# A block-sparse attention and gated feed-forward kernel: more buffers in eight tile groups, and a new order of all its instructions

## The chip, the cores and the metric

The kernel runs on one core of one Trainium2 chip. The metric is the device time of one execution in microseconds (us), as the median of several runs.

## The reference

The inputs are `q`, `k` and `v` of shape (4, 8, 768, 64), a table of sampled blocks, and the weights of a feed-forward layer. In short:

```python
scores = q @ k.T / 8                       # 4 batches, 8 heads, 768 x 768
mask   = near | first or last block row/column | 3 sampled blocks of 32 per block row
attn   = softmax(where(mask, scores, -1e9)) @ v
x      = heads side by side                # (4, 768, 512)
h      = relu(x @ w_in)                    # (4, 768, 1024)
gate   = sigmoid(conv3(h, conv_w))         # along the tokens, each feature by itself
out    = (h * gate) @ w_out                # (4, 768, 512)
```

## The kernel before

The batches are cut into halves of 384 query tokens, the last half again into 256 and 128, so that there are nine segments. The attention of a segment is cut into units of eight 128 x 128 score blocks; there are 144 units in all, numbered in the order of their exponentials. Two heads (a head pair) share a slot of tiles; there are 16 head pairs.

For each head pair, POOL's DMA queue loads keys and queries (`nat`, and `nq` for the second half of the queries of the first five pairs) and values (`vn`), with a cast to bf16. The first five pairs are transposed by TensorE into PSUM (`k_tr`, `q_tr`) and copied out by DVE or ACT; the later pairs are transposed by DMAs that SP issues (`xb`, into `stg`, L583) and copied by DVE (`stg_cp`). Both end in the tiles `e` and `o`, which also hold 24 rows that make the mask a part of the score matmul. The mask rows of slots 1 and 2 are copied by DVE, those of slots 3 and 4 by DMAs on SP (L359).

For each unit, PE makes the scores in two halves (`s`, L744, into one of two PSUM tiles `st`), ACT takes the exponential (`exp`, L755, into one of the `pt` tiles), and PE multiplies with V and a column of ones (`av`, L777). At the end of a head pair in a segment, DVE takes the reciprocal of the sums (`rcp`, L694) and normalises (`norm`, L696) into `xtok`; SP's DMA transposes that into `xT` (`x_xb`, L705), or PE does for a few (L715). When the four pairs of a segment are there, PE runs the first linear layer (`f1`, L893), ACT or DVE the relu (L913, L915), DVE the convolution (`mul`, `add`, L947, L957), ACT the tanh that stands for the sigmoid (L996), DVE the gate (`g1`, `g2`, L999, L1004), PE the second linear layer (`f2`, L823; L808 for the last 128 tokens), ACT or DVE the eviction (`ev`, L326 or L328, into `o2s`), and SP or ACT the store (L831, L817). One late segment's convolution runs on PE (L968), with diagonal matrices that DVE makes (`diag`, L388).

Nothing is scheduled when the program is built. All operations are collected in a graph, and a string `ORDER` is then replayed: two characters name an operation, one more its engine where there is a choice (P, A, V, G, S), and one more each buffer it takes. Each engine executes its own operations in the order of that string, and waits for operands and for the buffer's last reader.

```python
            o = ops[64 * CODE.index(line[x]) + CODE.index(line[x + 1])]
            ...
            if len(engines) > 1:
                e = ENGINES[line[x]]
            ...
            for b in o.allocs:
                b.index = CODE.index(line[x])
```

Loads on POOL are held back by small copies (`pace`): some read the loaded tile of three loads earlier (L658), the later ones an exponential (L415), so that a load is issued no earlier than that has happened. This rule is part of the graph, whatever the order.

The buffer counts stand in one line, from which the tiles are made:

```python
    NSLOT, NSTG, NNAT, NVN, NPT, NXK, NXT, NHE, NCV, NGT, NOS = 5, 2, 4, 3, 6, 3, 3, 2, 4, 2, 4
```

`NXK` counts two groups of tiles, `xtok` and `rcp`.

Of the kernel before, what the change touches and what calls it, by code (L numbers as in the profile page):

```python
# [25 lines left out]
1n15N05u5y5O5z05G0P470Q48241490R4a1A04b0S4c2604d274e0T4f2c24g1O14h2e14i2f4j2k04k2m34P05a4l2n4m5K35S15H5L5T5P4
5A25B5C1oV5U55/05M605Q6105R6415V5W656906a5X05Y25V41pV5Z05+V6616e16216fhr1ho06b26g36j0hp636khs0k0DhqV0htVhM06l4
6r1676s6t5hx0hyhzA6w06xhu1hv1B06y0hOhNhPhwVhQhU1hVhWhX6B16C686c6d6hhD16G0hE6H1CA1DA6D1hFAhA06i6m6n06O1hB1W16u
6P6v6z6I2hCAhRhY1XV46o1i021YV6pi16Q36T0hG06A6U6E6V4hH6F6Y16ZhJ16J6+56KhK710726R16S6WhZhLAhIA730i3hSi26L0i4hT0
i57611P1im06X6/1RV1QV777e01Z1707f747817j17k756M2806q1296Ni831+V1/Viah+2dV0h/i9ig17g27l37o07p797a07h7i7t17u7q4  # L30
i6ibi77b2ic7v5ih7B07C7D0id7m7n7r7s7G17w7x7Hin2lV12aV0io7L07M2g12h7I17N2ii7c7d7y12bV7z7E17Q17R7F7J7K7V07Wieifip
7O7S37A7X42s12u2v24n0IiqV0811827P7T7U860878358807Y7Z0ij8b18civ0iw8g08h7+02iV12jV2tV2ixV7/ikA1is1itiuViQ08d12o0
2p8i28o18p8q3iB08t0848uiC858v48y18z898a8e8f8D08E8j8kiy1iz8A58F12x2w2C2002F802iAAiRiSiTiDViU2qV2iV2rV8l2iY1iE0
8r18s8I18w8JiF8K0iGA8x8Q02118B8R8C8V18W8GiH0iI8H8S28X3iZi+22V8miW23Vi/8+08/904iXj0iJVj18LiK1iL931948M0iMVj42j5
8N1j7j28O8T9b08U8Y9ciN0iO8Z91iPVj39559g19h9d19i0jC19l09m9n3929697980jc3j6jdj8jfjejg999q19r9s59e19f9j9k9v09wjq0
9x19D19E9o9pjr9t9u9I0jD9y9J9z0j99F0jh9N19G9O9HjajbjijEjs9K59P02G02D22EV3jj2I2H2Q2N2R12O02y12z2J08n2K8P9a9S09T
jFjt9U2juA20L2LV39A2jGV32PV49B2MV2AV40K2BV9+19L9M9/a30a49QjI1jJa04jL0a819RjM9Va9a53jKA1jNA2/3032T2S2Yaa032ad0
aejU19Wa119X19YjX0k40jVai1a2jYaf1jWAk6jZVa6a7ajk11aq0abark2jO0acak2jPas5k5kk1k7kmjQAav1awaA0agahalaBjR0jSam0
ax4aC3k8k3Vklknan0j+1j/k0VkoaF1atjTAk9kc2aokdks3kfkakektkgkukb1aGaN0jk0auayaOaH0jlazaS1aTaP1kpaU5jw1jmaX0aYir
jHjv2U09C0il331aZ4khjxaDaEjnjoA0aIaJb01b1b23jyjzb50aQ1aRb6aVaWkA0jAA3b70kqaK22V2WV0kvkikwkjaLkxbd1a+bekG1a/b3  # L40
b4kBbi0bjkHb8b902Z131373820Map9Z34aMbf2bn1bo2XVkykrkCkzkD2+V0bk139V135V1bp536Vba0bb3a3b23f3c3d3ebs0kIbtkJkKV2
bA1kEA1kP0bBkQkM1kNkRVkOVl80l9lalblcbu4bC3bF0bGbgbhblbK1bLbmkS0bqbH0bM2bP0brbQkTbR1bU1kV1kWbVc00bvbwbD1bEc1ld
kUVkXVbx1lg2lhlelibyk/0bIbJbNbW5c23c51c6c70bOl0ca0cbbSbTbXbY0cf1cgkY1kZcc2ch5ljl1Vlklfk+VbZ2lllo13p3m3n03q03u
3r3g0bc1jp3hkFb+b/bzc3l20c4cn0cocp4l51l3l6cs1ctcx0l4Al7Acyc8c9lK0cdcecicjcu1cz3lplqlr3v1lw3lmlxlnlslylzcC1cD
cE0ltck0lAlucllvlE1cq1cH0lFcIcP1crcvcwcAcQcBcFlLcGcJ5cU0cKcL0cVlGlMlBcR4cW13s3E3t3B3F13J3G3H3C13I3Q3R2cmcScZ1
c+3iV2lClDlHlNd20d3cTc/2cXda1db3oV2lIV0cM2lOV1d43dc0m31cYd0m00d1m1m4cN3jVm2V0m5Adf0dgdk1dlm60m7dh5mo0mpm8Vdm4
mf1mgd5d6dp0dqdu1mc0mddr1meAmhAdd1jB3w3klP3K0cO23L3T3U33Y3V3W3Xdvdw2434403ldedC0dDml0mmm91mamnAdE3mr3xV4d71mq
3yVmsmE2dH1didImi0mjmFmGmbVmw1mxdJ0mkVmtd8djdM0dndodNlQ1dR1dSdslRdO5lSdtdxdZ0d+lTdT4mM3mHmz3DV3dz0mumydAmImv0
mAlUV3mNmOd/1e21e3dy0dFdGdKe70e42dLlW0lXdPdQe8ec1dUdVedmJmBe93lYlZe01m+1e1ee0mCdW2mDmPl+A1eh0eiej5e5e6m/eamU0
mVebep1eqeu0evmKmQdXmLmR3MV3mSmTn0mWn13Z1kL3+d93SV445V03/V0mXefegekdBlVdYl/3AlJer4ew1n2A2em13NVen40VmYA3ez1eA  # L50
eE0nd1eFeB2neeG3na0nbnfVncVnA0nBnCnDnE3PmZ3O3z41eo042eM1eNeO0el0n41eR0eSeT5n5n70n8eW1eseteXe/0exeyf0eCeDn6An9A
ns1eY4ng1nhf41eHeIf5nj0f11nFntnuniVeJ0nveKf62fc0nkfdfe3nwnlVnxnGnI2np1nqnJnrVnKnynLeP1fh1eQfinm0eUeVfm0eZfnnn
e+f2f3f7fj0fo5noAnznMnQ3nSnRnHf92nTfafr1f80fffsfgfkflfpfz0fAft4fB1nNnY1fE1fFo20fqfufvfJ0fKfG2fw1nUnOfL3nVfxnP
nZo3fR1fC1fDfHfSfIfMfW0fXfNn+o4fT0fY5eLfbfyf/1fU0g0nWg14nXo5o6V10Hg70g8n/fVfZgc1gdo0A0ok0olo7n3o1g91ge2fO0omV1
on1ooopVoI1oKgh0gioq0gp1gj3oJoLfPot1orosAgqouovAoQ0oRoToSgu0gvgr0oC0f+g2oF1oGoHAoDoEAgw5g3g42oUp42g5ga1gbgz1gA
oz1oAgfgggkglow0oxoBAgB4p5gm1oMgs0gnoyAoY3gtgxgyfQ1g6gogCgI0gJgDoNgN1gK1gOoe1ofogp6gE0gFoZo+gL1gG0gMgV0gP2gHV
o/oVp0oOoWohgQgWp7oP1gS2oiA3gR0po0ppgX3pqApA1gTp8h11h2pu1gYgZpvpx0pyh60h30pwApr1pspzAp1pBpCoXpQ0p2p3g+0pDg/ptA
p9papRpEpbpI3pJpLo80o9h7gU2h0hf1oaobhgh41h5h85ocA1pi1pjpkhh4plh9ha0hihjpc0pmA2pFhb1hchd1heAhk2pKhlpdpehm1pfpM
pNpgA0pGhnVqg1qhqiAqp0qqpHpY2pSpOpTqrAqj1qkqs1qtqm0qnqlAqu1qoAqx0qypPqz3pZp/pUpVp+qvq0phpnodojq1qa1qC1q40qDqH0
qIqwpWpXqJ1qE0q2qAqBq3qM0qbqcq5qFq6q7qdqeA0q8A2qfq9qKqGqLqNqOqPqQA1qRAqS1qTqUqVqWV3qXSqY0qZq+q/r0Ar1A  # L60
"""


# [49 lines left out]
def kernel(  # L113
# [210 lines left out]
    def dcopy(e, dst, src):  # L324
        if e == "ACT":
            nc.scalar.copy(out=dst, in_=src)  # L326
        else:
            nc.vector.tensor_copy(out=dst, in_=src)  # L328
# [732 lines left out]
```

## Time and profile before

| | |
|---|---|
| runs | 210.04, 211.36, 209.91 us; median 210.04 |
| profiled execution | span 207.2 us from the first to the last instruction |
| granted TensorE clock | 1.000 |
| PE, DVE, ACT, POOL busy | 95%, 88%, 91%, 29% of the span |
| DMA moved | 26.26 MB, mean 127 GB/s |

The time of a run is counted around the span; the profiled execution's own time is known only as its span. PE is TensorE's matmuls, PEld its weight loads, DVE the vector engine, ACT the scalar engine, POOL GpSimd, and SP the engine that only issues DMAs. A name like `st<-o,e` is the tile that is written and those that are read. L744 is line 744 of the kernel. "SPq" is SP's sequencer, issuing. In brackets stands how long an engine was idle before an instruction, and what ended that.

### The profile page before, as it was taken

The numbers are of one execution on the slowest core, as the hardware profiler recorded it, in microseconds if no ns is written. First come the engines' busy times: TensorE is split into PE (matmuls) and PEld (weight loads), VectorE is DVE, ScalarE is ACT, GpSimd is POOL, SyncE is SP. The second block draws the span as 40 slices with busy tenths as digits, with TensorE's granted clock in tenths as the row PEclk, the third lists the DMA queues.
The fourth block names the chain that finished last, engine by engine and source line by source line (L and its number), as shares of the span: only waits on it lengthen the run. The fifth ranks groups of instructions, "written<-read, shape, count | busy, mean of one in ns | idle before, by whom it ended". The sixth has DMA issues, their size and how long they took to land.

```text
span 207.2 us, 6783 instructions
## 1 busy us (share of the span) xinstructions
PE 196.7 (95%) x2667; PEld 153.7 (74%) x2687; DVE 181.5 (88%) x571; ACT 189.4 (91%) x248; POOL 60.7 (29%) x113
## 2 busy tenths in 40 slices
PE   7799979989999999999999999999999999999993
PEld 7689858867878877777688767777688877795752
DVE  6877759999699998999999998999799959999950
ACT  6899969999999999999999998999899999998841
POOL 8844355446326124500605292700000000000000
PEclk9999999999999999999999999999999999999999
DMA  6999999999998699993597689992511032100415
GB/s 149 170 207 200 173 169 126 141 135 157 158 151 134 98 138 194 181 190 58 77 167 133 88 103 218 170 213 73 175 43 22 19 121 66 29 11 6 156 50 202
DMA packets 54903, 26.26 MB, mean 127 GB/s; under 512 B 40864, under 2 KB 51832, under 8 KB 54872
## 3 DMA queue, kind: packets, MB, share of 16 engines
q0 software_dynamic: 19984, 11.24, 43.5%
q1 hardware_dynamic: 34312, 13.90, 33.8%
q10 hardware_dynamic: 576, 0.69, 1.0%
q8 instruction: 21, 0.34, 0.7%
q14 instruction: 10, 0.08, 0.2%
HBM read 23.08 MB, written 6.29 MB: 142 GB/s over the span
## 4 chain that ended last, share of the span: by engine, by line
PE 56%; ACT 16%; DVE 16%; DMA 5%; issue 4%; SPq 0%; ACTq 0%
PE st L744 16%; PE mix L893 14%; PE mix L823 14%; ACT pt L755 12%; PE av L777 9%; DVE m L947 5%; DMA xT<-xtok 3%; DVE m L957 3%; DMA o2s<-in_q_dram 2%; DVE hE L915 2%; DVE xtok L696 2%; DVE gT L1004 1%; ACT hE L913 1%; DVE m L999 1%; DVE e L328 1%
## 5 line engine op out<-in xcount | busy, mean ns | idle before, releaser
L755 ACT ACTIVATE pt<-st 128x1024 bf16<-128x1024 f32 x144 | 140.2, 1036 | 5.4 <-PE st L744 5.0
L777 PEld LDWEIGHTS <-pt 128*128 128x128 bf16 x1152 | 53.1, 97 | 11.6 <-issue 0.2
L777 PE MATMUL av<-vt,pt 128*128 128x65 bf16 x1152 | 60.6, 193 | 0.3
L893 PE MATMUL mix<-xT,winb 128*128 128x384 bf16 (+2 forms) x288 | 53.8, 308 | 1.1 <-DMA xT<-xtok 0.9
L947 DVE TENSOR_SCALAR m<-hE,cw 128x382 bf16<-128x382 bf16 (+2 forms) x192 | 49.6, 317 | 0.2
L744 PE MATMUL st<-o 88*128 88x128 bf16 (+1 forms) x240 | 44.3, 229 | 1.1 <-ACT pt L755 0.8
L744 PE MATMUL st<-o,e 88*128 88x128 bf16 (+1 forms) x228 | 43.8, 233 | 0.5 <-ACT pt L755 0.4
L744 PE MATMUL st<-e,o 88*128 88x128 bf16 (+1 forms) x224 | 43.0, 234 | 1.2 <-ACT pt L755 1.2
L823 PE MATMUL mix<-woutb,gT 128*128 128x512 bf16 x156 | 43.1, 379 | 0.8
L744 PE MATMUL st<-e 88*128 88x128 bf16 (+1 forms) x208 | 41.5, 239 | 0.6 <-ACT pt L755 0.5
L744 PEld LDWEIGHTS <-o 88*128 88x128 bf16 x464 | 34.4, 97 | 9.4 <-issue 3.0
L744 PEld LDWEIGHTS <-e 88*128 88x128 bf16 x436 | 33.0, 97 | 7.5 <-issue 1.4
L957 DVE TENSOR_TENSOR m<-m 128x764 bf16<-128x764 bf16 (+2 forms) x64 | 33.8, 532 | 0.4
L893 PEld LDWEIGHTS <-winb 128*128 128x128 bf16 x288 | 23.9, 97 | 8.2 <-issue 1.6
L996 ACT ACTIVATE m<-m 128x764 bf16<-128x764 bf16 (+2 forms) x32 | 26.3, 826 | 0.5 <-DVE m L957 0.4
L415 POOL COPY pace<-pt 1x1 bf16<-1x1 bf16 x24 | 8.3, 347 | 47.3 <-ACT pt L755 47.0
L823 PEld LDWEIGHTS <-gT 128*128 128x128 bf16 x184 | 15.4, 97 | 9.0 <-DVE gT L1004 0.5
L915 DVE TENSOR_SCALAR hE<-mix 128x384 bf16<-128x384 f32 x29 | 15.9, 554 | 4.3 <-PE mix L893 4.1
L696 DVE TENSOR_TENSOR xtok<-av,rcp 128x384 bf16<-128x384 f32 (+2 forms) x36 | 18.2, 506 | 0.3
L1004 DVE TENSOR_TENSOR gT<-m,hE 128x764 bf16<-128x764 bf16 (+3 forms) x36 | 18.1, 508 | 0.3
L913 ACT ACTIVATE hE<-mix 128x384 bf16<-128x384 f32 (+2 forms) x35 | 16.9, 503 | 1.6 <-PE mix L893 1.2
L238 POOL DMA_DIRECT2D nat<-in_q_dram x23 | 16.9, 736 | 3.0 <-issue 2.8
(80 smaller groups left out, 156.4 us busy)
## 6 DMA issues: line engine op xcount, KB each, us to landing
out_dram<-o2s SPq DMA_DIRECT2D x22, 256.0 KB
vn<-in_v_dram POOLq DMA_DIRECT2D x16, 192.0 KB, 5.3
...
xT<-xtok SPq DMA_TRANSPOSE x32
```

The costliest lines, as they stand in the source:

```text
L696: nm = op("norm", {"DVE": t_dps(128 * C)}, lambda e: nc.vector.tensor_tensor(out=xtok_t[xk.index][:, 0:C].rearrange("p c h d -> p h c d"), ...
L744: nc.tensor.matmul(out=st[:, 128 * x:128 * (x + n_)], lhsT=QK[kc % 2][s][0:88, 1, hh, kc // 2, :], rhs=QK[par][s][0:88, 0, hh, idx:idx + n ...
L755: nc.scalar.activation(out=pt_t[ptb.index], in_=st_t[stb.index], func=AF.Exp, bias=0.0, scale=0.125)
L777: nc.tensor.matmul(out=o[:, off:off + 65], lhsT=pt_t[ptb.index][:, 128 * x:128 * x + 128], rhs=V_t[vslot_b[P].index][:, hh, kc, 0:65], sta ...
L823: nc.tensor.matmul(out=acc(), lhsT=gT_t[gb.index][:, ffc, 128 * t:128 * t + 128], rhs=woutb[:, ffc, :], start=(ffc == 0), stop=(ffc == NFF ...
L893: nc.tensor.matmul(out=mix_t[hb.index][:, w1 * y:w1 * y + w1], lhsT=winb[:, fc, 128 * ffc:128 * ffc + 128], rhs=xT_t[xt_buf[n].index][:, f ...
L913: i = nc.scalar.activation(out=dst, in_=src, func=AF.Relu, bias=0.0, scale=0.5)
L915: i = nc.vector.tensor_scalar(out=dst, in0=src, scalar1=0.5, scalar2=0.0, op0=ALU.mult, op1=ALU.max)
L947: i = nc.vector.tensor_scalar(out=m_t[cb.index][:, x, y, 0:w], in0=hE_t[heb.index][:, f0 + y, t0 + x:t0 + x + w], scalar1=cw[:, x, f0 + y: ...
L957: nc.vector.tensor_tensor(out=m[:, a_, :, 0:w], in0=m[:, a_, :, 0:w], in1=m[:, b_, :, 0:w], op=ALU.add)
L996: th = [op("tanh", {"ACT": t_act(2 * w) + 0.04}, lambda e, cb=cb, w=w: nc.scalar.activation(out=m_t[cb.index][:, 0, :, 0:w], in_=m_t[cb.in ...
L1004: i = nc.vector.tensor_tensor(out=gT_t[gtb.index][:, f0:f0 + 2, t0:t1], in0=m_t[cb.index][:, 0, :, 0:w], in1=hE_t[heb.index][:, f0:f0 + 2, ...
```

## The change

Seven buffer counts grow: `stg` 2 to 3, `nat` 4 to 6, `vn` 3 to 4, `pt` 6 to 8, `xtok` and `rcp` 3 to 4, `xT` 3 to 4, and `o2s` 4 to 5. These are eight groups of tiles. The string `ORDER` is another one: it holds the same 1775 operations, in another order, with other buffers, and 45 of them stand on another engine. Of these, seven evictions go from ACT to DVE and two from DVE to ACT, four value copies go from DVE to ACT, and relus go both ways (nine to DVE, ten to ACT). The two PSUM pools for scores and accumulations keep their size. The copies of the mask rows into the other slots get one more dependency in the graph, on the first head's key rows; the copies read them in both versions.

```diff
@@ ORDER
-040708090506000b1e00a0A0102030e0c0z0d0gV1f1c01q11s11t0WV20f0hA0oA0UAr21r3r4r5r6r7r8r9rarbrcrdrerfrgrhrirjrkrl
...
+05040001020b0x030607r21r3180r4r50e08r6r7r8r9ra0a0crb1e0rc0gA0hVrdrerfrgrhri1frj0drk0oArlrmrnrorp1c00WA1rqrrrs
...
-    NSLOT, NSTG, NNAT, NVN, NPT, NXK, NXT, NHE, NCV, NGT, NOS = 5, 2, 4, 3, 6, 3, 3, 2, 4, 2, 4
+    NSLOT, NSTG, NNAT, NVN, NPT, NXK, NXT, NHE, NCV, NGT, NOS = 5, 3, 6, 4, 8, 4, 4, 2, 4, 2, 5
...
                 mr.append(op("m_slot", {"DVE": t_d4(1536) + 0.05}, lambda e, t=t, s=s: dcopy(e, t[s][64:88], t[0][64:88]),
-                             T(4.5 * s - 2.5) + 0.1 * x, [m_h1[x], m_kh[x]], earliest=7.0 + 2 * s))
+                             T(4.5 * s - 2.5) + 0.1 * x, [m_h1[x], m_kh[x], m_k[x]], earliest=7.0 + 2 * s))
             else:
                 mr.append(op("m_dma", {"SP": 0.75}, lambda e, t=t, s=s: nc.sync.dma_start(out=t[s][64:88], in_=t[0][64:88]),
-                             T(4.5 * s - 2.5) + 0.1 * x, [m_h1[x], m_kh[x]], dma=("hw", 0.6)))
+                             T(4.5 * s - 2.5) + 0.1 * x, [m_h1[x], m_kh[x], m_k[x]], dma=("hw", 0.6)))
```

The durations in the graph (`t_d4` and the like) are used by the search for an order, not by the program. What the new order does at the places that matter, engine by engine:

```
DVE, around the first normalisations
 before  rcp0 k_cp7 he_zero cw v_cp2 k_cp8 k_cp9 q_cp14 q_cp15 norm0 v_cp3 diag0 rcp1 diag diag norm1 q_cp5 q_cp4 rcp2 norm2
 after   rcp0 k_cp7 norm0 k_cp8 v_cp2 q_cp14 rcp1 q_cp15 norm1 k_cp9 q_cp8 rcp2 norm2
ACT, before the first exponential
 before  m_q m_h1 cast_q0 k_cp0 cast_k1 cast_q1 k_cp1 k_cp2 q_cp2 q_cp3 m_h1 exp0
 after   m_q m_h1 cast_k0 cast_q0 m_h1 k_cp0 q_cp1 q_cp0 cast_k1 cast_q1 k_cp1 exp0
POOL, first loads (pair numbers)
 before  k1 q1 v0 v1 k2 q2 v2 k3 q3 nq0 nq1 v3 w_in k4 q4 w_in
 after   nq0 k1 q1 v0 nq1 v1 k2 q2 v2 k3 q3 v3 w_in k4 q4 w_in
PE, around the first f1 (s: half units; f1.0 and f1.1: the two halves of feature block 0, and so on)
 before  s42 av36 s43 f1.2 f1.0 s44 f1.1 av37 s45 f1.3 s46
 after   s42 s43 f1.0 f1.1 f1.2 f1.3 s44 s45 f1.6 f1.7 s46
```

More of the change, by code (lines that the diff above doesn't have):

```diff
@@ L26 @@
[L26 to L60, printed above, removed]
+05040001020b0x030607r21r3180r4r50e08r6r7r8r9ra0a0crb1e0rc0gA0hVrdrerfrgrhri1frj0drk0oArlrmrnrorp1c00WA1rqrrrs
@@ new lines @@
+0frt0UArurv0nA1m10Y00B1210z0irwrx0ZA0ryrz1q1rA14ArBrC13ArD0jVrE0XArFrG0mV1s2rH4o00lV0VA0u4p0q0+A0/01trI4q0rJ
+15110V09rK4t116V4u1E20t17V1g10p4v14y01G34z0y11V1j00A1hV14A21H4D14E1lV1kV1S34F31dV04I04J1iV0O4r14s4K40s4Q11U44R
+0k4w4x4B4S54C464V01V0C4W0D1rV11u00r4X60P4+14/1vV21x1474G5070Q4H1yV530541zV4L4M04T5504N04U1wV5b15c4Y4O4Z515d152
+5g04P05h1I15i2565l11JV35m571L01FV25n35q01MV5r5e15815f1NV5j5s45k595v15w1KV5o5a5p1905x55D05E1n15t5F65u1oV5y5I1
+5A25J482405B5K75N01TV35O5C491pV0R5z01bV5P01aV5S15T0E15G5H5U15L5M5Q5/0605R6125V6415W655X35Y663690621634a1A05Z0
@@ new lines @@
+6a5+V6e16b40F6f0Gho04b0Shphr16g5hqV0hs6j025V44c2656khtAhx06l6hyhM06r1hN6shu14dhzA27hvhP6t76w0hOhD06xhQhEhwA6B1
+4e6y00ThFVhA16ChU16768280hR4fhBhW2c16c6dhV6hhCA6i1B0hS6G06D10w6m1CV6H1W16o01DV4g6n01O16p6I26u6O16PhX6q1hJ06Q3
+1XV46T06U1YV4h6v2e16zhK0v6V4hY6Y1hG1i024i29hH2fhZhLV6Z6A710hT0hIA6E1P04jh+6+52k2726F1QV1Z16J1RV6Ki83736761i177
+6R16S2g16Wi27874k2m07e07f6L1i96X6/707g0i37j17k2h4l6Mig02n7l1ia7o07p1+V744m6N75797q2i47a07t17u1/V7h7i7b37mib7v3
+7n7r7B07c7C7si5h/7d7w7xim17y27D47G17z7Hini67Aic7I5ihi77L07Mid2aV07E12o27Q17R2bVio7N6ieii2pif7F7J7S77V02iV17Wij
@@ new lines @@
+2jV7X0ipikV081182iqV12u8602s383187iv02dV0iw4n0M200is1882ixVit2v28b10K8ciuAiB02lV12x8d32w8g0iQ08h7KiR7Oiy18i4iC
+iS8o1iTiziDA7P2qV27T8piAA8t0iU8u8q5iK0iY17U7Y7Z0i+2y084iV85898y17+0iZ8ziL8v62rViN1iO7/8A78a8D0iW8028EiMV8e8f8j
+iPAi/8k8I18J8F0jc2iE0iFj08r18K18s8l12F8Q02G3jd8R8w211iGV8S28x8B8V12tV28WiX8C8Gj18H2I23ViH02C2D08miI8X38+022V8n
+8/2Hje8L8M08T8U905j2931iJV94jC18N32J1956j432N9b02O19cj68Y8Z9d7j59g12z9hj391929i08O9l09mj7968P97jq09n4982j89e1
+9f9j9q199j99r2Qjr2R4jf9a9v09s19wjgjDja9kjh2K9ojb9p9t9D19E9x2jEjiiljsjj9F39u0I2T9I09y9Jjt9K59N1juV29O9z0jF9P6
@@ new lines @@
+2AV39G9S09TjGV3jL09U79+12BV9H9/jI19A0a009B9LjJjM0N9C3a30jKA1jNVa42/3059M2EA3a819Qk40a92U29R2Sa549Vk59Wa11jR12Y
+jS2Z2aa1jU0jTVjVad0k6aejWA32jO131k7af2jP9X1jX09Yai1330jQAajk8aq0a2ak32PV4jYkc1arj+1keas6j/37383jZVav1awa62LV4
+k9a7abk10kdacagk0Aahkk3aA0alax7am0kmk234aBan3kfjw1k3AjxkaaC52MV2VataF1aGkgjk0aH0aoauaN0kljlapkhaOkb1aS1ayknjm
+aP4ks2azaTaDkoaEaIaU1jn2+V0aJkujykpaK2aX0kiaQ1aYaLaRjoA4aVb01ktaMb1aZ2jzkqkjkG0b23kvaW9Za+b50jAV0b6a/kHb76kw
+bd1jvbekrkA1jBkx3a35V0kB3b1irkCbf7kyb3bi0kzbjb42WV1kIbk5bn12XVbokJ0Jbp03fkD3ckKV2b8bs0kEA03dbtba0kLbA139V1kP0
@@ new lines @@
+bu436VkF3ebBkM1bbkQbC1bc0kNbF0kOVb90bGkRAbK1bLbH23g1l80kV1kWl9kS0bM3kXVbP0bQlbkTbR6bglabU1bVkUVbhblbmbW7lc3p
+c003q0c1bqlg1brbvbwc25bD1lhbEkY1bx3c51ljbIldbJ3uc6li3rk/0c70bNlkca03mkZ3n0lel0byllbO3scbl1VbSbzbTbXcc1cf1k+V3t
+cgl50lml21ch2lo33hl6lqcn0col7AlpbY0c3cs1cp43v2lnc4c8ctlfc9l3cu3lrcx0cybZ2cd3wlsl4AlE0cC1b+ltcecDlw2lFb/cz6lx
+lK1lycicjcq1crcE7ck1cv3ElzcH03F2cIcwcllLcJ5lAcAcmcP1cBlucFcQlBcG3JlvcK3GcU0cVcR0cL0lClG3H3oV2lMlDcW23BcZ13iV2
+c+lNcM0c/43K0lHlOV1d20d3lIA23xV3cScTcX3zda1d43cNcYdbd03yVm01cO1dc6d13jVm1m30m2V0m43TlPd53U3df0m5Vdgdk13C1m91
@@ new lines @@
+mo1dh7mampdl3Id6mqm60dm5m7mbVdd1dedid73dp0m8Vdj3Ydq3Vmrml1dr1du13Wmmmsdvmw0mf0mnA3Q3R2dC0mxdw0dDmgmz3Xdnmi1dE4
+d8mj43443domhVdsd9dH1dImtmkVdM0mc0mM3dJ3dtdxlJdNmNdy0lW13LmydO6dFmdmudGdR1mOdSmeA3Z2dZ0mAdKdT7dLdPmPd+dQlXmE2
+jpd/2lQ0mF3+lRmHmBe21e3mv0dUdVlYe45mGe70dz2lZdW1dA3DA3e8dXec1edl+A0mIe01dYe1e5lSe91mCmQlTmU1mDee0dBe63MV4eaeb
+eh0lUV1mJeiep13kmVmRmKeqefm+0mLer4m/mSn0mTej3mW3/V1mX40V3SA4eu1mYV2evegn145A0ekn71n2V4ew6ez0eA3NVn8eB7n40em0n5
+eneE1n6VeFn9Aeo2eM0eNeG2ns1na1nbntnd03AeO5nuneeR1nvl/eSncAel0nfVeset42eT1eW0nweXnj1nA0jHnkeY0ng0nC3lnhnlVe/1nx
@@ L61 @@
+gHAp43gX2gQgR1h10gS3h2p5pr0oiA1p0psgTojh61oXpo1ptAgU0p7ppp1p6h7gYgZpqAo80p8o9h35pI1oapA0obp2p9pChf0h40pJpu1
+ocA0g+0pvpah81g/px0pKh0h5pBhgpwApyp3hh0h9ha1pDodpi1pLpjhb1pzApbpkhchipEplpMhjpc0pmA2hk2pdhlpFpY2pnhm1pehnVpNp+
+hd1pfheVpQ3qg1pgA4pGqhpO0HqiAqj0qkpPqs0qtpSqlAqm1qnqu1pHqp0pZqx1qoAqqpRqyqC0qvq41qz0pTqrAqDqAq5p/pUqa0qwpVqbqB
+q0qH1qE1qIpWqM0q1pXqNqJ0q2qcq3q6qKqFqLqdqGq7qeV3qOq8A1qPqS0q9qQV0qTqUphqVqY1qRSqZqWA2q+q/qfr0AqXSr1A
 """
```

9 lines of the change are left out of this document (5 added, 4 removed).

## The prediction

> **What bounds the kernel now.** I read the page first, then the stretches of five us, the chain of waits, the timeline of the first 36 us, and the waits. Part 1 of the page:
>
> ```profile
> span 207.2 us, 6783 instructions
> PE 196.7 (95%) x2667; PEld 153.7 (74%) x2687; DVE 181.5 (88%) x571; ACT 189.4 (91%) x248; POOL 60.7 (29%) x113
> ```
>
> The span of the profiled execution is 207.2 us and the median of the runs is 210.04, so 2.84 us lie around the span. I keep that distance and make the sum against 207.2. Three engines are near full, so no share of the whole names the bound. The stretches do (time; PE, PEld, DVE, ACT, POOL busy with counts; PE clock; DMA share; GB/s):
>
> ```profile
> 15.00:20.00 5.00, 4.78 (x85) 4.55 (x83) 3.85 (x13) 5.00 (x7) 2.44 (x5) 1.00 1.28 197
> 25.00:30.00 5.00, 3.84 (x55) 2.87 (x52) 2.32 (x10) 4.33 (x5) 2.61 (x6) 1.00 1.25 166
> 45.00:50.00 5.00, 4.57 (x79) 3.92 (x79) 4.96 (x17) 5.00 (x7) 3.43 (x4) 1.00 1.39 148
> 130.00:135.00 5.00, 5.00 (x64) 3.77 (x62) 4.94 (x18) 5.00 (x8) 3.24 (x6) 1.00 1.29 155
> 195.00:200.00 5.00, 4.95 (x47) 3.18 (x46) 4.58 (x20) 3.24 (x8) 0.00 (x0) 1.00 0.52 193
> ```
>
> ACT is full at 15 and at 45. At 25 all three engines drop at once, which is a latency that nothing covers. At 130 all three are full, and at the end PE alone is. The chain of waits (start, length, what) says the same in order of time:
>
> ```profile
> 8.57 5.39 ACT pt L755 x6
> 22.73 6.50 DMA xT<-xtok
> 29.27 0.65 PE mix L893 x3
> 71.50 1.35 DVE m L947 x6
> 114.85 0.92 DVE m L947 x4
> 131.64 1.30 PE mix L893 x8
> 189.19 1.73 PE mix L823 x8
> ```
>
> So there are four regimes: ACT's exponentials until about 22 us; one landing of a transposed attention tile (xT) from 22.73 to 29.23; ACT again to about 62; then PE, with two spells of DVE near 71 and 115. PE's matmuls in the chain stand end to end (8 of 512 columns in 1.73 us, 0.216 each), so nothing but idle PE time can be won there.
>
> **The change part by part.** No operation is added or removed but two pad memsets. Seven buffer counts grow and every engine's order is new, and 45 operations change engine. PE, where the work is the same to the instruction, can only lose waits.
>
> *Before the first exponential.* ACT's rows:
>
> ```profile
> 3.61 0.51 ACT L326 COPY o<-o 24x384 bf16<-24x384 bf16 x1
> 5.11 0.51 ACT L326 CAST nat<-o2s 128x384 bf16<-128x384 f32 x1
> 6.12 0.35 ACT L326 CAST nat<-o2s 128x192 bf16<-128x192 f32 x1 [0.50 <-DMA o2s<-in_q_dram]
> 6.50 0.47 ACT L326 COPY o<-mix 64x384 bf16<-64x384 bf16 x1
> 7.00 0.74 ACT L326 COPY e<-av 64x384 bf16<-64x384 bf16 x2
> 7.75 0.26 ACT L326 COPY o<-av 64x128 bf16<-64x128 bf16 x1
> 8.03 0.51 ACT L326 COPY e<-e 24x384 bf16<-24x384 bf16 x1
> 8.57 20.79 ACT L755 ACTIVATE pt<-st 128x1024 bf16<-128x1024 f32 x22
> ```
>
> Before the exponential at 8.57 stands a mask copy (8.03) that the first exponential doesn't need. The new order puts it earlier, into time that ACT spent waiting, gives ACT the first key cast, and gives DVE the three copies of the second head. From the end of the copy at 3.61, 4.12 us, ACT then runs two casts of 0.51, two of 0.35, the mask copy 0.51, two key copies of 0.47 and two query copies (0.37 + 0.26): 3.80 us, to 7.92. That is 0.65 earlier.
>
> DVE has to follow. For the third head pair it now has a short mask and the second head's copies (three, that took ACT 0.74 + 0.26) ahead of it and two query copies and a cast less, roughly as much more as the 0.77 that it waited there:
>
> ```profile
> 14.40 0.55 DVE L328 COPY e<-mix 64x768 bf16<-64x768 bf16 x1 [0.77 <-PE mix L468]
> 15.39 0.42 DVE L328 COPY e<-mix 64x512 bf16<-64x512 bf16 x1
> ```
>
> These copies ended at 15.81 and would again end near 15.8, while the tenth exponential could run at 7.92 + 9 x 0.90 = 16.0 (5.39/6 by the chain's row). Its scores start when the copies end; half a unit of them and the hand-over put it at about 16.4: some 0.4 of the 0.65 may be given back. I keep 0.3.
>
> *The first attention tile.* This is the largest single term. Normalising the first head pair (L696) stood behind mask, value and key copies and behind nine diagonals; SP's three transposes went out after it:
>
> ```profile
> 15.73 0.18 DVE L694 RECIPROCAL rcp<-av 128x6 f32<-128x6 f32 x1
> 19.88 0.56 DVE L696 TENSOR_TENSOR xtok<-av,rcp 128x384 bf16<-128x384 f32 x1
> 21.21 1.25 DVE L388 TENSOR_SCALAR diag<-ident,cw 128x128 bf16<-128x128 bf16 x6
> 23.59 0.56 DVE L696 TENSOR_TENSOR xtok<-av,rcp 128x384 bf16<-128x384 f32 x1
> 20.46 4.97 SPq L705 DMA_TRANSPOSE xT<-xtok  x3
> 29.27 0.65 PE L893 MATMUL mix<-xT,winb 128*128 128x384 bf16 x3 [0.87 <-DMA xT<-xtok]
> 30.91 1.94 ACT L755 ACTIVATE pt<-st 128x1024 bf16<-128x1024 f32 x2 [1.55 <-PE st L744]
> ```
>
> In the new order only one key copy stands between that reciprocal and its normalisation: it runs near 17 instead of 19.88, the second near 19.5. The third, with nine diagonals (1.25 for six, so 1.9) out of its way, runs near 21.8 instead of 23.59. With a fourth xtok buffer the fourth needn't wait for a transpose. The second transpose, issued at 22.73, landed 6.50 us later; issued near 19.8 it lands by 26.3. The third goes out near 22.4. If it too takes 6.5 it lands at 28.9; if it takes 5.0 it lands at 27.4. Then come eight f1 matmuls at 0.16 us (0.216 x 384/512, which the 0.65 for the last three agrees with) and one unit's scores before the exponential that was at 30.91. It would run between 30.5 (gain 0.4) and 29.0 (gain 1.9). I take 1.2, near the middle, since one duration is measured at 6.5 and the queue ahead holds the same bytes. The 0.3 of the start lies inside this, since f1 then waits for the landing and not for ACT. PE's 0.87 us at 29.27 and ACT's 1.55 are the same stall and count once.
>
> *ACT until unit 54.* From the first exponential on, ACT now has two relus more and an eviction and the pair of q copies at 34 us less:
>
> ```profile
> 34.01 0.59 ACT L326 COPY o<-mix 64x512 bf16<-64x512 bf16 x1
> 34.60 0.37 ACT L326 COPY e<-mix 64x256 bf16<-64x256 bf16 x1
> L913 ACT ACTIVATE hE<-mix 128x384 bf16<-128x384 f32 x27 | 12.9, 505 | 0.8 <-PE mix L893 0.6
> L326 ACT COPY o2s<-mix 128x512 f32<-128x512 f32 x15 | 8.7, 592 | 3.3 <-PE mix L823 3.2
> L328 DVE COPY o2s<-mix 128x512 f32<-128x512 f32 x7 | 4.8, 682 | 2.3 <-PE mix L823 1.6 <-PE st L744 0.7
> L328 DVE COPY vt<-vn 128x768 bf16<-128x768 bf16 x16 | 5.6, 359 | 0.1
> L996 ACT ACTIVATE m<-m 128x764 bf16<-128x764 bf16 x16 | 13.5, 850 | 0.0
> ```
>
> That is 2 x 0.505 - 0.592 - 0.59 - 0.37 = -0.54 us, on the engine that is full there: a gain of 0.5. Over the whole program ACT loses five evictions (-2.96) and gains four value copies. A value copy on ACT has no row: 768 elements lie between 0.505 (384) and 0.85 (764), nearest the latter, so 4 x 0.85 = 3.4, and from 2.0 as the other end. ACT as a whole stays level within about 1 us. DVE gains five evictions (5 x 0.682 = 3.4) and loses the value copies (4 x 0.359 = 1.4): about +2.0. It idles 25.7 us, so I cost that at nothing; with that cover gone it is the rival below.
>
> *Loads and the other buffers.* The second-half queries of pairs 0 and 1 move to the front of POOL's queue, so the loads of pairs 1 to 3 follow one or two places later, some 0.74 us an issue (736 ns in the first row below). DVE's 0.77 at 14.40 ended with PE's transposes and not with a load, so the loads were there before, and I cost this at nothing; with that cover gone it is 0.74 for each place. The fourth value load no longer waits for a copy, since it has a fourth vn buffer; that is off the path. Staging and os buffers let SP and the evictions go on earlier, which nothing in the chain waits for. The eight pt buffers and the looser order could pay in the second of these rows:
>
> ```profile
> L238 POOL DMA_DIRECT2D nat<-in_q_dram x23 | 16.9, 736 | 3.0 <-issue 2.8
> ACT pt L755 <- PE st L744: 5.0, 11, 1.6
> ```
>
> ACT waits 5.0 us for scores, 1.55 of it at the first tile, so 3.45 in the middle. Counted in exponentials, the new order keeps more distance in it: attention-times-V within the same unit as its exponential falls from 31 cases to 16, a multiply in the unit of its relu from 68 to 11. I take a third of 3.45, 1.1; the ends are a gain of 3.4 and a loss of 1.5 (the size of the largest stall that a new order could open).
>
> The Perfetto Trace Analysis page of the Trainium skill (Optimization Strategy, under Identifying Performance Opportunities) says that a gap which repeats on the engine that should be saturated can mean too few buffers. ACT's repeated gap waits for scores in PSUM, whose two st tiles are not enlarged; by that reading the added buffers give none of the 1.1, and the sum would be 1.1 us higher. No run yet shows another count, so the trace neither agrees nor disagrees.
>
> *The sum.* 1.2 + 0.5 + 1.1 = 2.8 us: a span of 204.4, a time of 207.2 us. The tail holds the same work in nearly the same order, and counts nothing.
>
> **The rivals.** *The landing doesn't move.* Loads fill the DMA engines at 15 to 30 us (share 1.28 and 1.25 in the rows above), and the same bytes are ahead of f1. Then earlier transposes only wait longer: f1 starts at 29.3 as before, and the 0.5 is left with nothing from the middle. 209.5 us. Against it: what is measured is a time from the issue, so an earlier issue should move the landing. DMA: Bandwidth & Descriptors of the Trainium skill (Issuing engines are not separate DMA queues) says that all issuers share the same 16 engines and interleave; the 6.50 us of one transpose among loads agrees with that.
>
> *DVE becomes the bound.* It is 88% busy, and sets the chain near 71 and 115 us. Five more evictions stand in its queue just where gates are made, with relus and gates behind them, for which PE's f2 waits. If DVE's total decides, the head gain is lost, because DVE has no less to do, and 2.0 is added: 212.0 us, and it decides from the point at which DVE idles less than about 20 us between 30 and 200. Against it: PE's rows near 131 and 189 run end to end with DVE not in the chain.
>
> *A landing comes late in the middle.* By its description the order was found with landings counted from the issue. Where a queue is fuller than that assumes, a transposed stage (`stg`) or xT comes late, the in-order copy on DVE or f1 on PE stops, and everything behind it stops too, as at 22.73. The place is the turn of a batch, where loads, stages and xT meet in SP's queue (units 36, 72, 108). Three stalls of the size seen on ACT (1.55) against the gains outside the middle (1.7): 210.04 - 1.7 + 4.65 = 213.0. It decides from two such stalls on. Against it: the shortest distance from stage to copy grows in the new order, to four units.
>
> **How the numbers follow.** Forecast 0.54, its own range 204.9 (middle gain 3.4) to 209.8 (middle loss 1.5). Landing unmoved 0.14, DVE bound 0.16, late landing 0.16. A measurement of this kernel can tell about 1% from no change, 2.1 us: below 207.9 is faster, above 212.1 slower. The forecast gives 0.48 faster and 0.06 within; the first rival 0.02 faster, 0.10 within, 0.02 slower; DVE 0.07 within and 0.09 slower; the late landing 0.02 within and 0.14 slower. Together 0.50, 0.25, 0.25. The range that holds 8 in 10 runs from 203.8 to 212.8: it takes in the DVE rival and most of the late landing's cases.
>
> **What would show it.** Right: the first exponential near 7.9; the first transpose issued near 17; f1 beginning before 28.5 with no DMA wait; the exponential after it at 29 to 30.5; ACT's wait for scores under 4 us in all. Wrong: a DMA wait still standing at f1; DVE busy above 90% with ACT or PE waiting for gates; new idle time of PE beyond 1.5 us at one place between 60 and 190.

## The result, and the profile after

The changed kernel takes 212.17 us, the median of 17 runs (211.11 to 213.76), against 210.04 us before: a ratio of 1.0115, with an interval from 1.0085 to 1.0146. By that ratio it is about 1.2% slower, 2.4 us; the two medians lie 2.1 us apart. The forecast was 207.2 us and faster. The profiled execution of the changed kernel took 212.35 us with a span of 210.6 us. Executions of both kernels scatter by some per cent; the ratios leave disturbed ones out, and where the profile of an experiment (e3, e5, e8, e13) is of one of its longer executions, only the places in it are used, not its length.

Parts 1 and 2 of the page of the changed kernel (the DMA line is the share of the DMA engines in 40 slices of 5.27 us, in tenths):

```profile
span 210.6 us, 6783 instructions
PE 197.1 (94%) x2668; PEld 153.0 (73%) x2687; DVE 183.5 (87%) x575; ACT 189.3 (90%) x246; POOL 57.7 (27%) x113
DMA  6999989999793996997796987999023215211106
```

PE, DVE and ACT are as busy as before within 2 us (196.7, 181.5 and 189.4), so the 3.4 us of added span are waiting. About one of them lies in the choice of execution: with the same 1.75 us outside its span, the profiled execution of before took some 208.95 us, 1.1 below its median. Two stretches of both kernels say where (time; PE, PEld, DVE, ACT, POOL busy with counts; PE clock; DMA share; GB/s), first of before:

```profile
2.00:50.00 48.00, 43.39 (x662) 37.22 (x662) 39.78 (x129) 45.35 (x61) 27.50 (x50) 1.00 1.27 167
50.00:70.00 20.00, 19.95 (x286) 16.05 (x287) 18.06 (x52) 20.00 (x25) 7.15 (x13) 1.00 1.00 145
```

and of the changed kernel:

```profile
2.00:50.00 48.00, 41.25 (x643) 35.00 (x642) 35.97 (x117) 42.99 (x57) 25.55 (x49) 1.00 1.25 168
50.00:70.00 20.00, 19.79 (x268) 15.18 (x266) 19.70 (x58) 19.34 (x24) 5.71 (x12) 1.00 0.82 112
```

Until 50 us the DMA engines move the same 8.0 MB in both (48 us at 167 and 168 GB/s), with a share above 1: on average an engine had more than one packet under way. But PE was busy 2.14 us less, ACT 2.36 and DVE 3.81 (some 1.5 of that are six diagonals that the new order makes later). The same bytes came in, and less could be done with them. From 50 to 70 us PE loses only 0.16 more. The loss sits in two stretches of four us: PE is busy 1.92 us between 28 and 32 (before 3.13) and 1.81 between 40 and 44 (before 3.49). The starts of some exponentials, read from the traces in us, follow this through the program:

```
unit                          0     21     22     31     42     48     54     143
before                      8.57  28.33  30.91  44.29  55.19  61.23  68.96  189.28
changed kernel              7.87  27.93  31.75  45.28  57.56  65.42  71.94  191.93
changed, nq3 earlier   e3   7.89  27.96  31.09  42.57  54.76  66.49  73.18  193.57
changed, f1 later      e4   7.88  28.06  28.96  44.08  56.36  64.61  71.14  191.68
changed, order of need e6   7.88  28.04  29.86  41.24  53.42  68.97  75.26  195.40
changed, order of need e9   7.89  28.06  29.45  40.91  53.28  63.63  71.64  191.37
changed, 1 MB less    e11   7.88  28.19  29.52  41.15  53.56  61.43  67.95  187.39
before, order of need e10   8.26  28.03  30.39  43.78  54.68  60.72  68.44  188.78
```

The new order leads by 0.7 us at the first exponential and 0.4 at unit 21. It is behind by 0.8 at unit 22 and by 3.0 at unit 54. From unit 54 to unit 143 both take the same: 120.3 us before and 120.0 after.

The chain of waits (start, length, what) names the two places:

```profile
22.04 7.99 DMA xT<-xtok
30.08 1.14 PE mix L893 x6
36.48 7.00 DMA nq<-in_q_dram
43.53 0.41 PE mix L506 x4
51.92 2.69 DMA xT<-xtok
```

Before, the one landing in the chain was the second transpose (6.50 us from 22.73). Now it is the third one, 7.99 us after its issue at 22.04, and then the load of the second-half queries of pair 3 (nq3), 7.00 us after its issue. Before, the third transpose was issued at 24.23, and f1.1, which reads it, ran at 29.98 without a wait:

```profile
24.23 1.21 SPq L705 DMA_TRANSPOSE xT<-xtok  x1
29.98 0.49 PE L893 MATMUL mix<-xT,winb 128*128 128x384 bf16 x2
```

So it had landed by 29.98. Issued 2.2 us earlier in the changed kernel, it landed at 30.03, no earlier. The waits (engine, line, what; us, times, longest) have both as TensorE's own:

```profile
ACT pt L755 <- PE st L744: 5.1, 8, 1.8
PE mix L893 <- DMA xT<-xtok: 2.3, 1, 2.3
PE mix L506 <- DMA nq<-in_q_dram: 2.2, 1, 2.2
```

Before, the first of these DMA waits was 0.9 us, and the second did not exist on PE (0.3 on its weight loads).

### The profile page after: what moved, and what is told of

It reads as the page before. It is cut to its first block, busy times and chain, and to the rows that moved or that the text cites. A ratio compares the mean times of both kernels' runs of the same rounds, so it can differ in the third digit from the quotient of the medians.

```text
span 210.6 us, 6783 instructions
## 1 busy us (share of the span) xinstructions
PE 197.1 (94%) x2668; PEld 153.0 (73%) x2687; DVE 183.5 (87%) x575; ACT 189.3 (90%) x246; POOL 57.7 (27%) x113
## 4 chain that ended last, share of the span: by engine, by line
PE 51%; DVE 20%; DMA 12%; ACT 10%; issue 3%; POOL 1%; ACTq 0%; POOLq 0%; DVEq 0%; SPq 0%
PE st L744 17%; PE mix L893 12%; PE mix L823 11%; PE av L777 8%; DVE m L947 6%; ACT pt L755 5%; DMA xT<-xtok 5%; DMA nq<-in_q_dram 3%; DVE m L957 3%; DVE xtok L696 2%; DMA stg<-nat 2%; DVE gT L1004 2%; DMA nat<-in_q_dram 1%; DVE o L328 1%; DVE e L328 1%
## 5 line engine op out<-in xcount | busy, mean ns | idle before, releaser
L777 PE MATMUL av<-vt,pt 128*128 128x65 bf16 x1152 | 59.0, 193 | 0.3 <-ACT pt L755 0.2
L777 PEld LDWEIGHTS <-pt 128*128 128x128 bf16 x1152 | 51.4, 97 | 9.6 <-ACT pt L755 0.6
L947 DVE TENSOR_SCALAR m<-hE,cw 128x382 bf16<-128x382 bf16 (+2 forms) x192 | 50.5, 321 | 0.3
L744 PE MATMUL st<-e,o 88*128 88x128 bf16 (+1 forms) x224 | 42.3, 234 | 0.6 <-ACT pt L755 0.4
L744 PEld LDWEIGHTS <-e 88*128 88x128 bf16 x436 | 33.5, 97 | 9.1 <-issue 1.6
L913 ACT ACTIVATE hE<-mix 128x384 bf16<-128x384 f32 (+2 forms) x36 | 17.6, 499 | 3.5 <-PE mix L893 3.4
L415 POOL COPY pace<-pt 1x1 bf16<-1x1 bf16 x24 | 6.3, 264 | 52.5 <-ACT pt L755 52.5
L915 DVE TENSOR_SCALAR hE<-mix 128x384 bf16<-128x384 f32 x28 | 15.2, 553 | 5.4 <-PE mix L893 5.3
```

Of the source, the lines that this page charges most:

```text
L744: nc.tensor.matmul(out=st[:, 128 * x:128 * (x + n_)], lhsT=QK[kc % 2][s][0:88, 1, hh, kc // 2, :], rhs=QK[par][s][0:88, 0, hh, idx:idx + n ...
L777: nc.tensor.matmul(out=o[:, off:off + 65], lhsT=pt_t[ptb.index][:, 128 * x:128 * x + 128], rhs=V_t[vslot_b[P].index][:, hh, kc, 0:65], sta ...
L913: i = nc.scalar.activation(out=dst, in_=src, func=AF.Relu, bias=0.0, scale=0.5)
L947: i = nc.vector.tensor_scalar(out=m_t[cb.index][:, x, y, 0:w], in0=hE_t[heb.index][:, f0 + y, t0 + x:t0 + x + w], scalar1=cw[:, x, f0 + y: ...
```

## The experiments

Theory A is that landings in the first 55 us set the pace: the DMA engines are full, a transfer lands when what is in flight beside it has landed, and the new order asks for two or three of them too early. Theory B is that the new order of the work on PE, ACT and DVE is worse in itself. Loads are named as in the change (w_out0 to w_out3: the four loads of the second weight matrix).

**e1: the buffers alone.**

```diff
-    NSLOT, NSTG, NNAT, NVN, NPT, NXK, NXT, NHE, NCV, NGT, NOS = 5, 2, 4, 3, 6, 3, 3, 2, 4, 2, 4
+    NSLOT, NSTG, NNAT, NVN, NPT, NXK, NXT, NHE, NCV, NGT, NOS = 5, 3, 6, 4, 8, 4, 4, 2, 4, 2, 5
 ORDER: the order of before; each operation takes the buffer that has been free longest
```

> The order of before, engine by engine, unchanged; only the buffer counts are those of after, with each tile taken from the buffer that has been free longest. Theory (two landings make the loss): the extra buffers are no part of it, ratio to before 0.996 to 1.004. Rival (the buffers themselves, by other places in SBUF or by letting loads bunch): ratio 1.008 or more. Rival (the buffers are a gain that the order spoils): 0.992 or less.

Measured: 0.9988 (0.9950 to 1.0025). The buffers alone do nothing that can be measured in the order of before.

**e2: the early normalisations alone.**

```diff
 DVE, order of before
-rcp0 k_cp7 he_zero cw v_cp2 k_cp8 k_cp9 q_cp14 q_cp15 norm0 v_cp3 diag rcp1 diag diag norm1
+rcp0 k_cp7 norm0 he_zero cw v_cp2 k_cp8 k_cp9 q_cp14 q_cp15 v_cp3 rcp1 norm1
```

The nine diagonals follow behind `norm2`.

> The order of before with the first normalisation behind the first pair's last key copy, as in after, the second behind its reciprocal, and the nine diagonals behind the third. Theory (a transpose lands with the loads that were issued with it): transposes go out 1.5 to 3.5 us earlier, but the one that f1 waits for lands within 1 us of 29.2; ratio 0.995 to 1.004. Rival (the landing follows the issue by a fixed time, as the prediction had it): f1 starts near 27.5 without a DMA wait, ratio 0.988 to 0.994.

Measured: 1.0018 (0.9986 to 1.0051): nothing gained, and the rival's 0.988 to 0.994 lies outside the interval. Its profile can't be read for the landing, since TensorE ran at half its clock from 11 to 18 us and everything after came late.

**e3: one load of the changed kernel earlier.**

```diff
 POOL
-w_out0 v4 w_out1 nq2 w_out2 k5 q5 w_out3 v5 nq3 k6
+w_out0 v4 w_out1 nq2 nq3 w_out2 k5 q5 w_out3 v5 k6
```

> The kernel after, with one load moved on POOL: the second-half queries of pair 3 right behind those of pair 2 (five loads earlier). Theory: the wait of 2.2 us on PE at 43.5 goes, exponential 31 runs near 43.4 instead of 45.3, and 1.2 to 2.0 us of the loss go with it; ratio to before 1.001 to 1.006. Rival (the loss lies in the middle, from DVE's evictions or the order): the wait goes, and the time stays within 0.4 us of after, ratio 1.009 to 1.014.

Measured: 1.0029 (0.9981 to 1.0076). The wait for nq3 is gone from the profile and unit 42 starts at 54.76, ahead of before. Before unit 48 the next landing is missing, a transposed stage. From the chain and the waits (its lines are numbered one higher, so L329 is L328):

```profile
55.27 7.14 DMA stg<-nat
DVE e L329 <- DMA stg<-nat: 4.0, 2, 2.6
```

What came back in time is uncertain. By the ratio it would be 0.9% of the 1.15%, but its twelve executions lie between 209.23 and 218.40 us, and their median of 212.39 against 209.96 before is no better than the changed kernel's. The profiled one (214.00 us) lost the gain again to the stage, at a clock of 1.00.

**e4: f1 later, so that its late transpose delays nothing else.**

```diff
 PE, changed kernel
-s42 s43 f1.0 f1.1 f1.2 f1.3 s44 s45 f1.6 f1.7 s46
+s42 s43 s44 s45 s46 s47 f1.0 f1.1 f1.2 f1.3 f1.6 f1.7
```

The exponentials of units 22 and 23 move ahead of the relus.

> The kernel after, with two more units of scores on PE ahead of the first f1 (and the first two relus behind their exponentials on ACT). Theory: exponentials 22 and 23 run near 29 and 30 instead of 31.8 and 33.0, but the second-half queries of pair 3 land at 43.5 as before and exponential 31 waits for them, so nothing is left at the end: ratio 1.008 to 1.014. Rival (the first stall alone makes the loss): ratio 1.000 to 1.006.

Measured: 1.0122 (1.0087 to 1.0157). Unit 22 starts 2.8 us earlier than in the changed kernel, unit 31 only 1.2, and the end 0.25. The next landing takes the room up: nq3 lands 6.32 us after its issue at 35.97, and PE waits 1.4 us for it.

**e5: the mask copies early.** In the changed kernel two of the four mask copies stand in SP's queue among the stages and transposes (start, length, what):

```profile
34.65 1.21 SPq L583 DMA_TRANSPOSE stg<-nat  x1
35.92 0.77 SPq L359 DMA_DIRECT2D o<-o  x1
38.30 1.21 SPq L705 DMA_TRANSPOSE xT<-xtok  x1
39.56 0.76 SPq L359 DMA_DIRECT2D e<-e  x1
```

```diff
 SP
-m_dma1 cw m_dma0 x_xb0 x_xb1 x_xb2 xb0 m_dma3 x_xb3 m_dma2 xb1
+m_dma1 cw m_dma0 m_dma3 m_dma2 x_xb0 x_xb1 x_xb2 xb0 x_xb3 xb1
```

> The changed kernel with its last two mask copies (L359, seen on SP's queue at 35.9 and 39.6 us among the transposes) put back ahead of the first transpose. Theory A (late landings in the first 60 us make the loss; these copies sit in the queue of the transposes at the worst time): the transposes behind them issue 0.5 to 1.5 us sooner, the query load of pair 3 lands at 43.0 instead of 43.5, and the time falls a little, ratio to before 1.006 to 1.011. Theory B (the loss is in the order of the work on TensorE, ScalarE and VectorE, whatever lands when): no change, 1.009 to 1.014.

Measured: 1.0112 (1.0068 to 1.0155). That is theory B's forecast rather than theory A's, though the interval takes in both; no cost of these copies can be seen.

**e6: loads in the order of need** (and e5's edit).

```diff
 POOL
-w_out0 v4 w_out1 nq2 w_out2 k5 q5 w_out3 v5 nq3 k6 q6 v6 k7 q7
+v4 nq2 nq3 k5 q5 w_out0 w_out1 w_out2 v5 w_out3 k6 q6 v6 k7 q7
```

> The changed kernel with the loads in the order of need (v4, the second query halves of pairs 2 and 3, then k and q of pair 5, and only then the four loads of the second weight matrix, which is first read near 46 us) and the mask copies early. Theory A: no wait for the third transpose (f1 starts before 28.5 us and runs on), none for the queries of pair 3 (in by 33), so most of the 3 us lost by unit 54 comes back: ratio to before 0.992 to 1.003. Theory B: 1.009 to 1.014 as the changed kernel.

Measured: 1.0186 (1.0133 to 1.0240). Both forecasts failed in size, but the profile is the clearest of all. By unit 42 it is 4.1 us ahead of the changed kernel and 1.8 ahead of before. Then it loses everything at one place:

```profile
53.16 4.87 DMA xT<-xtok
58.07 1.76 PE mix L893 x5
```

I had put the k load of pair 6 behind w_out3. It landed at 47.8, and the stage that waits for it stood at the head of SP's queue. DVE came to the copy of that stage at 50.86 and waited 3.54 us. Two evictions stood behind the copy, and PE needed the PSUM tiles that they free:

```profile
54.40 0.81 DVE L328 COPY e<-stg 64x1536 bf16<-64x1536 bf16 x1 [3.54 <-DMA stg<-nat]
55.87 1.26 DVE L328 COPY o2s<-mix 128x512 f32<-128x512 f32 x2
56.59 0.65 PE L893 MATMUL mix<-xT,winb 128*128 128x384 bf16 x3 [3.75 <-DVE o2s L328]
58.07 1.44 PE L893 MATMUL mix<-xT,winb 128*128 128x384 bf16 x4 [0.82 <-DMA xT<-xtok]
```

The late transpose in the chain, which stood behind the stage in SP's queue, cost PE another 0.82 us. What followed was not foreseen: the granted clock.

```profile
54.00:58.00 4.00, 0.65 (x3) 0.29 (x3) 3.56 (x8) 0.44 (x1) 2.55 (x4) 0.90 1.44 197
58.00:64.00 6.00, 5.93 (x33) 3.71 (x33) 3.66 (x14) 2.61 (x4) 0.00 (x0) 0.50 1.24 151
```

**e7: the same loads in the kernel before.** POOL's queue as in e6, with the order of work and the buffers of before.

> The kernel before with the loads in the same order of need, its order of work and its buffers untouched. Theory A: its own short waits for landings go (1.2 us at the second half of f1, under 1 us at the queries of pair 3): ratio 0.990 to 0.998. Theory B: 0.998 to 1.002, since its order of work already fits.

Measured: 0.9965 (0.9929 to 1.0001). That is in theory A's range, but the interval reaches into theory B's. From the first exponential to unit 22 it takes 21.87 us against 22.34, but to unit 42 47.04 against 46.62. Its k load of pair 6, too, is issued late (40.9 us, before 38.5); that this is what takes the gain away wasn't shown.

**e8: only w_out0 and w_out1 later.**

```diff
 POOL, changed kernel
-w_out0 v4 w_out1 nq2 w_out2 k5 q5 w_out3
+v4 nq2 w_out0 w_out1 w_out2 k5 q5 w_out3
```

> The changed kernel with nothing but the first two loads of the second weight matrix moved behind the query load of pair 2, out of the time in which the three transposes are under way (issue near 28 instead of 14 and 22 us). Theory A (a transpose lands when what is in flight with it has landed): the third transpose lands 1.5 to 3 us sooner, by 28.5, and f1 runs without a wait for it; the query load of pair 3 is as late as before, so the time stays at 1.008 to 1.013. Rival C (a transpose of this shape takes its 6.5 to 8 us whatever else is under way): it still lands near 30.

Measured: 1.0047 (1.0011 to 1.0084). This is less than the 1.008 to 1.013 that was expected for the time. The edit did not clear the way as expected: w_out0 went out at 22.07, right beside the third transpose, and w_out1 at 26.39. The third transpose was issued at 22.08, as before the edit (22.04), and f1 went on at 28.42 instead of 30.08 (timelines of SP, POOL and PE):

```profile
22.08 1.18 SPq L705 DMA_TRANSPOSE xT<-xtok  x1
22.07 0.72 POOL L238 DMA_DIRECT2D woutb<-in_moe_w_out_dram  x1
26.39 0.71 POOL L238 DMA_DIRECT2D woutb<-in_moe_w_out_dram  x1 [0.27 <-issue]
27.29 0.49 PE L893 MATMUL mix<-xT,winb 128*128 128x384 bf16 x2
28.42 1.14 PE L893 MATMUL mix<-xT,winb 128*128 128x384 bf16 x6 [0.63 <-DMA xT<-xtok]
```

The same transpose, with the same issue, landed 1.7 us sooner with one weight load of 256 KB fewer issued up to then (and nq2's 96 KB more). The other traces give the scatter. With the changed kernel's loads up to nq2, in e3 and e5, it lands at 29.36 and 30.22, 7.30 and 7.86 us after its issue. With the weight loads behind nq2, in e6 and e13, it lands at 28.14 and 28.86, after 5.99 and 6.70. In all six executions it lands 0.2 to 1.6 us after the load that was issued last before it. That falsifies rival C and the way the prediction counted. In this profiled execution the next landing, nq3, is later still (7.79 us, PE idle for 4.1), and the clock falls as in e6:

```profile
36.10 7.79 DMA nq<-in_q_dram
40.00:45.00 5.00, 1.07 (x11) 1.01 (x12) 0.93 (x3) 0.89 (x1) 2.14 (x6) 0.81 1.70 119
45.00:48.00 3.00, 3.00 (x39) 2.81 (x37) 2.94 (x12) 2.02 (x2) 1.63 (x3) 0.50 1.30 171
```

**e9 and e10: a second order of need**, e9 on the changed kernel (with e5's edit, and the stage of pair 5's queries ahead of the fourth transpose), e10 on the kernel before with nothing else changed.

```diff
 POOL
+v4 nq2 nq3 k5 q5 w_out0 w_out1 v5 k6 q6 w_out2 w_out3 v6 k7 q7
```

> The changed kernel with its loads in the order of need, as in the run before of that kind, but with k and q of pair 6 ahead of the third and fourth load of the second weight matrix, the mask copies early, and the second half of pair 5's stage ahead of the fourth transpose on SP. In the earlier run the k load of pair 6 issued at 43.0 and landed at 47.8; the stage behind it held SP's queue and with it the sixth transpose (landed 58.0), for which TensorE then waited 7 us at unit 42, after it had been 4 us ahead of the changed kernel. Theory A (landings and the queue behind them make the loss, not the order of work): unit 42 near 53.5 again (57.6 in the changed kernel, 55.2 before), no 7 us wait after it, ratio 0.980 to 1.000. Theory B (order of work): the lead is lost again by unit 54 at other places than a landing, ratio 1.006 to 1.014.

> The kernel before with the same new order of loads; its order of work, its buffers and its SP queue untouched. Theory A: it loses 1.2 us at f1 and under 1 us at the queries of pair 3 to landings, so 0.990 to 0.998. Theory B, or that other work takes up the room at once as in the earlier run of that kind (lead of 0.5 us at unit 22, gone by unit 41): 0.996 to 1.002.

Measured: e9 1.0175 (1.0092 to 1.0259; its six executions lie between 211.84 and 217.66 us), e10 0.9918 (0.9880 to 0.9956). The 7 us of waiting in e9's expectation are too many: in e6 PE waited 3.75 and 0.82 us there, as shown above, and then ran at half its clock. Unit 42 of e9 is at 53.28 as theory A said. But now k7 and q7 stand behind w_out2 and w_out3, and their stage comes late:

```profile
37.11 7.74 DMA woutb<-in_moe_w_out_dram
47.74 5.37 DMA nat<-in_q_dram
53.17 6.39 DMA stg<-nat
```

The lead is lost at a landing, as in theory A, but the forecast of the ratio was wrong. e10, in contrast, is faster than both kernels. Its runs lie between 207.92 and 209.91 us, those of before beside it between 209.31 and 214.43. The two profiled executions show little of that: from the first exponential to unit 54 it takes 60.18 us against 60.39, and the execution of before is one of its shortest, as said above. So that it is faster is measured; that it is by fewer late landings is theory A's reading of it.

**e11 and e12: 1.0 MB less to move.** The four loads bring 2 KB each instead of 256 KB, and f2 reads slices of the first weight matrix; e11 is the changed kernel, e12 the one before.

```diff
-woutb[:, 2 * x:2 * x + 2],
+woutb[0:1, 2 * x:2 * x + 2],
...
-rhs=woutb[:, ffc, :]
+rhs=winb[:, ffc % 4, 0:512]
```

> The changed kernel with its four loads of the second weight matrix cut from 256 KB to 2 KB each (one partition of 128); the second matmuls of the FFN read slices of the first weight matrix instead, same shape, so the second product is left out of the reference's sense, and all else is as it was. This takes 1.0 MB out of some 9.4 MB that move in the first 60 us, 6 to 7 us of transfer at the 150 GB/s of that stage. Theory A (the transfers of the first 60 us set the pace, and the changed order of work asks for its landings too early for them): the waits at f1 and at the queries of pair 3 go, unit 48 comes 3 to 5 us sooner than 65.4, ratio to before 0.975 to 1.002. Theory B (the order of work itself is worse): the landings are sooner but the time stays at 1.006 to 1.014.

> The kernel before with the same cut of the four loads. Theory A: its chain between 43 and 62 us goes through ScalarE, not through a landing, so it has less to win: ratio 0.988 to 0.997, and the gap between the two kernels, 2.4 us with the full loads, shrinks to under 1 us or turns round. Theory B: 0.996 to 1.002 and the gap stays above 2 us.

Measured: e11 0.9866 (0.9818 to 0.9915), e12 0.9924 (0.9879 to 0.9970). The difference between the two kernels is gone. In e11 all of the first eight f1 matmuls run at 27.51 without a wait, unit 48 starts at 61.43, 4.0 us sooner than in the changed kernel, and PE is busier than in either original:

```profile
27.51 1.47 PE L893 MATMUL mix<-xT,winb 128*128 128x384 bf16 x8
2.00:50.00 48.00, 45.94 (x686) 38.34 (x687) 40.23 (x126) 47.01 (x61) 24.86 (x49) 1.00 1.22 158
```

Every operation stands where the changed kernel has it, so the order of work isn't slow by itself: theory B falls as the whole cause. The edit does more than take bytes away, since lighter loads also let the later ones out sooner (nq3 at 33.63 instead of 36.48); it does not tell the two apart.

**e13 and e14: a third order of need**, on the changed kernel (with e9's other edits) and on the one before.

```diff
 POOL
+v4 nq2 nq3 k5 q5 w_out0 w_out1 v5 k6 q6 k7 q7 w_out2 w_out3 v6
```

> The changed kernel with its loads in order of need a third time: k and q of pair 7 too ahead of the third and fourth load of the second weight matrix (in the run before of that kind they issued at 46.9 and 47.7 and their stage landed at 59.6, which cost 2.2 us of waiting and after it some 4 us at a granted clock of 0.55 to 0.59); mask copies early and pair 5's second stage early as there. Theory A: with every landing in time the order of work of the changed kernel is as good as that of before with 1.0 MB less to move (ratio 0.987), at most a few tenths behind it: 0.986 to 1.000. Rival (what stands ahead of a load decides only which one is late: the DMA engines are full until 55 us, so another landing is late in its turn): 1.000 to 1.018.

> The kernel before with the same third order of loads and nothing else. The second order gave 0.9918 with the chain between 43 and 62 us free of landings, so there is little left for landings to give: 0.989 to 0.996 by theory A; by the rival one of the weight loads (third and fourth) is now the late one, 0.996 to 1.006.

Measured: e13 0.9983 (0.9935 to 1.0031), e14 0.9922 (0.9895 to 0.9949). With another order of its loads the changed kernel takes the time of before: the loss is undone with the order of work kept. (The median of all its twelve executions is 211.10, against 210.79 before.) It is no faster, and its profiled execution again has a late stage:

```profile
45.81 8.34 DMA stg<-nat
```

e10 and e14, at 0.992, are the fastest versions with the full computation: the kernel before, with its loads in the order of need. With the same order of the full loads the changed kernel is behind each time: e6 against e7, e9 against e10, and by least, 0.6% with intervals that overlap, e13 against e14. So its order of work stands up where no landing stops it (e11); why it loses more than the old one under the same full loads was not tried.

## Why the prediction was wrong

The head of the program came as worked out. The first exponential is at 7.87 us (forecast 7.92). The first three normalisations run at 16.02, 19.06 and 21.46 (near 17, 19.5 and 21.8), and the transposes are issued at 16.60, 19.64 and 22.04 (near 17, 19.8, 22.4). Of the 0.7 won at the start (forecast 0.65), 0.4 are left at unit 21 (0.3 kept).

**The step that failed is the landing of the third transpose in "The first attention tile".** It was given 5.0 to 6.5 us from its issue, so 27.4 to 28.9, and a gain of 1.2. It took 7.99 us and landed at 30.03, together with a weight load issued 0.3 us before it (at 21.72, landed at 29.87), and the term became a loss of 0.8. A duration measured among other transfers was used as if it belonged to the transpose. Issued 2.2 us earlier than before, this transpose landed no earlier (30.03 against 29.98 at the latest). e8 shows what sets it: with the issue unchanged, another order of the loads around it took 1.7 us off. This is the mechanism of the rival "The landing doesn't move", which had 0.14. It put f1 at 29.3 as before; in fact it was worse, since the new order runs f1.1, which needs the third transpose, ahead of the next scores, where the old one ran two halves that don't. e4 took that away and won nothing at the end, because of the next failure.

**"I cost this at nothing" was wrong for the loads.** The check was that the pairs' first loads were there in time. The one that was not is nq3, near the end of the same queue, where each load waits for the landing of an earlier one. PE came to it at 41.34 and waited until 43.53. Before, it landed at 42.11, and PE's weight load had already waited 0.3 us for it, so there was no cover at all. e3 takes this wait away by moving that load alone, though it is uncertain what time that saves. The two mask copies in SP's queue, which the prediction did not mention, show no cost (e5).

**The middle gave nothing.** ACT's wait for scores was to fall under 4 us and is 5.1 (5.0 before); units 54 to 143 gain 0.3 us in all, with DVE's and the buffers' terms in it. What ACT's 0.5 until unit 54 was worth can't be seen beside the 3.0 lost there. The prediction's reading of the Trainium skill's page Perfetto Trace Analysis (Optimization Strategy), by which these buffers give none of the 1.1 us, is the one that e1 bears out in the order of before, with 0.9988.

**DVE did not become the bound**: 183.5 us busy, 2.0 more as worked out, 87% of the span. "A landing comes late in the middle" had the right mechanism and the wrong places: at units 22 and 30, where one landing is waited for each time, not at the turns of batches (the 2.69 us from 51.92 in the chain is the only one near unit 36).

A smaller step: the distance of 2.84 us between span and time was taken from the median of other runs. The changed kernel's own is 212.35 - 210.6 = 1.75. By that the sum would have been 206.2, no nearer.

What stays open: whether the new order of work can win anything with the full loads. Without 1 MB of them it reaches unit 54 in 60.1 us from its first exponential, against 60.4 before, but each of the five orders of the full loads that were tried (e3, e6, e8, e9, e13) left a landing late in its profiled execution: nq3 in e8, a stage in the others.
